# A spectral filter and two MLPs on one core: the first batch's loads and stores reordered, its filter loads cut to the rows in use

## Chip, cores, metric

The kernel runs on one core of a Trainium2 chip. The metric is the device time of one execution in microseconds. The two kernels are measured on the same chip; the median of three runs of the kernel before is 1429.06 us (1428.6 to 1431.17).

## What is computed

```python
# x: (4, 3136, 256) f32; filt: (1569, 256) complex
y = irfft(rfft(x, axis=1) * filt, n=3136, axis=1)        # filter over the sequence
u = y + real(fft(fft(y, axis=1), axis=2))                # 2-D transform mixed in
u = u + relu(norm(u) @ w1a) @ w2a                        # MLP 1: 256 -> 1024 -> 256
out = u + relu(norm(u) * g @ w1b) @ w2b                  # MLP 2: 256 -> 1024 -> 256
```

`norm` subtracts the mean of a token's 256 features and divides by their standard deviation. All of it is float32.

## The kernel before

The sequence transform of length 3136 = 64 x 49 is done in two stages that meet in device memory. The first stage (`over_p`, a generator that yields after each step) multiplies x by a 128x128 constant in 13 steps: load x (L254), one product on TensorE (L302), copy out of PSUM on ScalarE (L332, into `gst`), store to the scratch tensor `g` in device memory (L333). The second stage (`over_q`) runs over 17 groups of frequencies. In its tick t it loads a piece of `g` (L265, tile `gr`), multiplies it by the second constant (L302, and from t = 2 on by a rotated copy, L408), multiplies by the filter on VectorE (L416, L418 or L420), adds on GpSimd (L422, writes `y`), takes differences (L458, writes `z`), and two ticks later does the inverse product (L302 with `y`) and the transposes (L439); ScalarE copies the results out (L444 or L446 into `vst`, L450) and stores `vst` (L373) to a second scratch tensor `v`. ScalarE also multiplies one half of each filter tile by a sign (L368). After the last tick `v` is loaded back (L495) and 25 units of 512 tokens (`prep_ticks`, `ln_ticks`, `w1_step` L682, `w2_step` L705) follow. Batches 1 to 3 go through both stages in the gaps of the units of the batch before, so only batch 0's transform, the subject of the change, stands by itself at the start.

The filter of batch 0 comes in 17 loads (`load_f`, tile `fc`), 16 of 512 KB and one of 256 KB; each fills 128 partitions, of which 0 to 48 and 64 to 112 hold values and the other 30 zeros. The first three go to pool `fp`, the next two to pool `up` (which holds x before), the last 12 to the memory of the weights `w2a`, `w1b` and `w2b`, which are written only later. A filter is loaded four ticks before its use, a piece of `g` three before.

The weights come as 64-bit words and are made into two float32r halves by `conv_ticks` in chunks of 512 columns: a load (L636, tile `ww`), three masks and two combining steps on VectorE (L665 to L667, L651, L653), three copies on ScalarE (L658, L659, L219) and two steps on GpSimd (L655, L220). One "a" step of the schedule moves the first three chunks of `w1a` on by one of these stations.

The order is written out by hand: every engine runs its instructions in the order in which the program issues them. `DURING` says after which half tick of `over_q(0)` which other steps are issued: `a` as above, `k` a load of constants (L730), `c` the other weight chunks, `s` the split of constants, `x` the loads of batch 1's x, `f` a step of batch 1's first stage. `P0` does the same during `over_p(0)`.

Loads are issued by SyncE (SP) in that order; `vst` is stored by ScalarE. A DMA raises one of eight semaphores, which are given out in turn, in program order, over both issuing engines. Before an engine issues a DMA it waits until the last one on the same semaphore has landed, so at most eight are under way, and an engine whose next DMA has to wait issues nothing behind it.

Of the kernel before, what the change touches and what calls it, by code (L numbers as in the profile page):

```python
# [9 lines left out]
F32 = mybir.dt.float32  # L10
F32R = mybir.dt.float32r
I32 = mybir.dt.int32
ACTF = mybir.ActivationFunctionType
# [4 lines left out]
B, S, D, H = 4, 3136, 256, 1024  # L18
# [109 lines left out]
NA, LAG = 3, 3  # L128
N1 = 8
AHEAD, XW = 4, 7  # L130
WHEN = (-1, -1, 0, 1, 3, 3, 4, 5)
DURING = {0: 'aa', 2: 'a', 6: 'a', 14: 'k', 16: 'a', 30: 'cs', 33: 'x', 35: 'ff', 36: 'sf', 37: 'cc', 39: 'f', 40: 'f'}
P0 = {9: 'a'}
AFTER = "ppcfspfcppfpfppfpppc"
CONV = (0, 1, 3, 6, 9, 11, 12, 14, 15, 17, 19, 20, 21, 22, 23, 24, 25, 26, 27, 28)
P1 = (2, 3, 4, 5, 7, 8, 9, 10, 10)
# [11 lines left out]
def spectral_mlp_kernel(ctx: ExitStack, tc, x, ff, cst, w1a, w2a, gln, w1b, w2b, out):  # L148
    nc = tc.nc
# [107 lines left out]
    def pairs(t):  # L257
        return t.rearrange("(j p) d -> p j d", p=128)
# [3 lines left out]
    def load_g(b, c):  # L262
# [2 lines left out]
        nc.sync.dma_start(out=t[:98], in_=src)  # L265
        g_raw[b, c] = t[:98]

    def load_f(b, i, eng=nc.sync):
        k0, k1 = XCH[i]
        nk = k1 - k0  # L270
        if b == 0 and i > 2:
            if i < 5:
                t = up.tile([128, 4, D], F32, tag="u", name="fc").rearrange("p a d -> p (a d)")
            else:
                j = i - 5
                if j % 4 == 0:
                    f_tile[0] = wp.tile([128, 4096], F32, tag="w" + ("2a", "1b", "2b")[j // 4], name="fc")
                t = f_tile[0][:, j % 4 * 1024:j % 4 * 1024 + 1024]
            t = t.rearrange("p (a t d) -> p a t d", t=2, d=D)
            eng.dma_start(out=t[:, :nk], in_=ff[:, k0:k1])  # L280
            f_sb[b, i] = t[:, :, 0], t[:, :, 1]
        else:
            t = fp.tile([128, 2, 2, D], F32, tag="f", name="fc")
            eng.dma_start(out=t[:, :nk], in_=ff[:, k0:k1])
            f_sb[b, i] = t[:, :, 0], t[:, :, 1]
# [19 lines left out]
    def over_p(b):  # L305
# [7 lines left out]
        def exact(c):  # L313
            return b == 0 or b == 1 and c < N1
# [5 lines left out]
        def store():  # L320
            k, n, ps = done.pop()
            if b == 0 and k % 5 > 2:
                st = vrp.tile([128, 2, D], F32, tag="vr", name="gst")
            elif b == 1 and exact(k):
                if k % 2:
                    st = tp.tile([128, 2, D], F32, tag="t2", name="gst")
                else:
                    st = hp.tile([128, 512], F32R, tag="hl", name="gst").bitcast(F32)
                    st = st.rearrange("p (a d) -> p a d", d=D)
            else:  # L330
                st = stg.tile([128, 2, D], F32, tag="st", name="gst")
            nc.scalar.activation(out=st[:, :n], in_=ps[:, :n], func=ACTF.Copy)  # L332
            (nc.sync if exact(k) else nc.scalar).dma_start(out=pairs(g_dram[b][k * 256:k * 256 + n * 128]), in_=st[:, :n])  # L333

        for c in range(NC):
            if c + 3 < NC and (b, c + 3) not in x_raw:
# [386 lines left out]
    with tc.manual_schedule():  # L723
        def load_consts(c0, c1):
            if c0 % 512 == 0:
                i = c0 // 512
                t = hp.tile([128, 512], F32R, tag="h" + "hhl"[i], name="cr").bitcast(F32)
                cf[i] = t
            t = cf[c0 // 512][:, c0 % 512:c0 % 512 + c1 - c0]
            nc.sync.dma_start(out=t, in_=cst[:, c0:c1])  # L730
            return t
# [16 lines left out]
        def bufs_b(kind, i):  # L748
# [9 lines left out]
                return flat(yp.tile([128, 2, D], F32, tag="y", name="wm"))  # L758
            return flat(zp2.tile([128, 2, D], F32, tag="z", name="we"))

        load_consts(0, 128)
        p0 = over_p(0)
        for c in range(XW):
            load_x(0, c)
        cv = conv_ticks(["1a"], bufs_a, lambda i: -1 if i < 2 else 1, 0, NA)
        run(cv, 1)
        for c in range(XW, 13):
            load_x(0, c)
        run(p0, 1)
        load_consts(128, 512)  # L770
        nc.sync.dma_start(out=ctail, in_=cst[:, nw - 128:nw - 128 + ctail.shape[1]])
        nc.sync.dma_start(out=g_sb, in_=gln)
        ar = zp2.tile([128, 2, D], F32, tag="z", name="ar")[:, 0]
        nc.sync.dma_start(out=ar, in_=cst[:, NCONST - D - 128:NCONST - 128])
        turned[0] = xnp.tile([128, D], F32, tag="xn", name="f2s")[:, :128]
        nc.sync.dma_start(out=turned[0], in_=cst[:, NCONST - 128:])
        cs = consts()
        q0 = over_q(0)
        k = 0
        while run(p0, 1):  # L780
            k += 1
            for what in P0.get(k, ""):
                run(cv, 1)
        load_f(0, 0)
        load_consts(512, 1024)
        for what in DURING.get(0, ""):
            run(cv, 1)
        nc.scalar.activation(out=alt, in_=ar, func=ACTF.Copy)
        nc.scalar.activation(out=zmid, in_=ar, func=ACTF.Copy, scale=0.0)
        p1 = over_p(1)  # L790
        act = {
            "a": lambda: run(cv, 1),
# [8 lines left out]
        k = 0  # L801
        while run(q0, 1):
            k += 1
            for what in DURING.get(k, ""):
                act[what]()
        load_v(0)
        p = prep_ticks(0)
        for what in AFTER:
            act[what]()
# [2 lines left out]
        nc_ = sum(v.count("c") for v in (*DURING.values(), AFTER))  # L812
        assert nf >= 2 + N1
        assert sum(v.count("s") for v in (*DURING.values(), AFTER)) == 3
        assert sum(v.count("a") for v in DURING.values()) + sum(map(len, P0.values())) >= NA + LAG


        blocks = [(0, 0)]
# [156 lines left out]
```

## Time and profile before

| what | value |
|---|---|
| median of 3 runs | 1429.06 us |
| the profiled execution | 1427.74 us |
| its span (first to last instruction) | 1425.9 us |
| TensorE matmul busy | 1384.6 us, 97% of the span |
| VectorE, ScalarE, GpSimd busy | 885.6, 622.7, 408.3 us |
| data moved by DMA | 123.66 MB, mean 87 GB/s |

The prediction's sum is made in the profiled execution; its own time lies 1.84 us above its span and 1.32 us below the median. Busy times are averages over stages that have different limits: TensorE is idle for 41 us in all, and nearly all of that lies in the first tenth of the span, where the DMA engines are busy throughout.

### The profile page before, as it was taken

Reading aid. Unit: us, or ns where it says so; the run is one execution under the profiler, and the core shown is the slowest. Engines: PE = TensorE matmul, PEld = TensorE weight load, DVE = VectorE, ACT = ScalarE, POOL = GpSimd, SP = SyncE. Lnnn points to the kernel's source line nnn. Section 1 sums busy time; section 2 is a strip of 40 time slices with the busy share of each in tenths; the row PEclk is TensorE's granted clock in tenths of the full one; section 3 lists DMA queues with packets and bytes.
Section 4 is the critical chain, followed back from the end, with each engine's and each line's share of the span. In section 5 each row is a group of like instructions: output and inputs, shape, how many; then the busy total and the mean of one; then the engine's idle time right before and its main releaser. Section 6 shows DMA issues by size and latency. Waiting matters only on the chain.

```text
span 1425.9 us, 22918 instructions
## 1 busy us (share of the span) xinstructions
PE 1384.6 (97%) x8835; PEld 1221.6 (86%) x8835; DVE 885.6 (62%) x1814; ACT 622.7 (44%) x1350; POOL 408.3 (29%) x361
## 2 busy tenths in 40 slices
PE   4978999999999999999999999999999999999998
PEld 2437899888989999898999998898999999999998
DVE  2779977777554775767545666667555555555453
ACT  4755545645444544545344355445333233323222
POOL 1635534535231333434032244334100010100000
PEclk7988999999999999999999999999999999999999
DMA  9973332422233313312233233131000000000000
GB/s 325 316 272 108 102 99 83 141 78 85 77 115 124 97 49 114 109 48 68 68 103 118 77 90 114 42 114 62 19 30 30 31 1 31 30 15 16 30 15 23
DMA packets 65981, 123.66 MB, mean 87 GB/s; under 512 B 6096, under 2 KB 32848, under 8 KB 65872
## 3 DMA queue, kind: packets, MB, share of 16 engines
q1 hardware_dynamic: 49920, 99.00, 21.6%
q10 hardware_dynamic: 15952, 23.20, 5.0%
q8 instruction: 69, 1.13, 0.3%
q14 instruction: 40, 0.33, 0.1%
HBM read 83.12 MB, written 39.06 MB: 86 GB/s over the span
## 4 chain that ended last, share of the span: by engine, by line
PE 88%; DVE 5%; DMA 1%; issue 1%; ACT 0%; POOL 0%; ACTq 0%; POOLq 0%; DVEq 0%
PE ps L705 37%; PE ps L682 36%; PE ps L216 11%; PE ps L611 3%; DMA vd<-vst 1%; PE ps L439 1%; DVE we L651 1%; DVE wm L653 0%; DVE hl L688 0%; DVE wm L666 0%; DVE ww L667 0%; DVE xn L602 0%; PE ps L549 0%; POOL rs L598 0%; PE ps L302 0%
## 5 line engine op out<-in xcount | busy, mean ns | idle before, releaser
L687 ACT ACTIVATE hh<-ps 128x512 fp32r<-128x512 f32 (+1 forms) x400 | 235.4, 589 | 689.3 <-PE ps L682 666.9
L688 DVE SCALAR_TENSOR_TENSOR hl<-ps,hh 128x512 fp32r<-128x512 f32 (+1 forms) x400 | 271.7, 680 | 424.5 <-ACT hh L687 423.3
L682 PE MATMUL ps<-xth,w1a 128*128 128x512 f32 (+1 forms) x800 | 247.0, 391 | 0.0
L682 PE MATMUL ps<-xth,w1b 128*128 128x512 f32 (+1 forms) x800 | 243.7, 386 | 0.0
L705 PE MATMUL ps<-w2a,hh 128*128 128x256 f32 x1568 | 221.3, 283 | 2.0 <-ACT hh L687 2.0
L705 PE MATMUL ps<-w2b,hh 128*128 128x256 f32 x1568 | 218.3, 281 | 0.0
L705 PEld LDWEIGHTS ps<-w2b,hh 128*128 128x128 f32 x1568 | 206.2, 188 | 10.5
L705 PEld LDWEIGHTS ps<-w2a,hh 128*128 128x128 f32 x1568 | 205.3, 189 | 10.9 <-ACT hh L687 2.4
L598 POOL TENSOR_TENSOR rs<-rs,mhalf 128x4 f32<-128x4 f32 (+1 forms) x51 | 50.4, 988 | 413.8 <-DVE rs L597 405.6
L682 PE MATMUL ps<-xtl,w1a 128*128 128x512 f32 (+1 forms) x400 | 156.4, 391 | 0.0
L682 PE MATMUL ps<-xtl,w1b 128*128 128x512 f32 (+1 forms) x400 | 155.7, 389 | 0.0
L682 PEld LDWEIGHTS ps<-xth,w1a 128*128 128x128 f32 x800 | 136.8, 190 | 18.0 <-ACT xth L219 0.5
L682 PEld LDWEIGHTS ps<-xth,w1b 128*128 128x128 f32 x800 | 135.2, 188 | 16.5
L705 PE MATMUL ps<-w2a,hl 128*128 128x256 f32 x784 | 123.4, 279 | 3.8 <-DVE hl L688 3.8
L705 PE MATMUL ps<-w2b,hl 128*128 128x256 f32 x784 | 122.0, 277 | 0.1
L422 POOL TENSOR_TENSOR y<-y,t 128x512 f32<-128x512 f32 (+1 forms) x67 | 87.2, 1302 | 99.8 <-DVE t L420 85.7
L705 PEld LDWEIGHTS ps<-w2a,hl 128*128 128x128 f32 x784 | 104.9, 189 | 4.3 <-DVE hl L688 4.3
L705 PEld LDWEIGHTS ps<-w2b,hl 128*128 128x128 f32 x784 | 103.9, 188 | 0.3 <-DVE hl L688 0.3
L220 POOL TENSOR_TENSOR sl<-gr,sh 98x512 fp32r<-98x512 f32 x48 | 63.3, 1318 | 109.7 <-ACT sh L219 107.8
L220 POOL TENSOR_TENSOR sl<-y,sh 128x512 fp32r<-128x512 f32 (+1 forms) x51 | 67.2, 1317 | 79.9 <-issue 59.1
L682 PEld LDWEIGHTS ps<-xtl,w1a 128*128 128x128 f32 x400 | 75.8, 190 | 15.1
L682 PEld LDWEIGHTS ps<-xtl,w1b 128*128 128x128 f32 x400 | 75.3, 188 | 14.4
(115 smaller groups left out, 2040.6 us busy)
## 6 DMA issues: line engine op xcount, KB each, us to landing
fc<-in_ff SPq DMA_DIRECT2D x61, 512.0 KB
vd<-vst ACTq DMA_DIRECT2D x64, 200.0 KB
gr<-gd SPq DMA_DIRECT2D x64, 196.0 KB
xr<-in_x SPq DMA_DIRECT2D x48, 256.0 KB
vr<-vd SPq DMA_DIRECT2D x48, 256.0 KB
out<-u SPq DMA_DIRECT2D x24, 512.0 KB
gd<-gst ACTq DMA_DIRECT2D x28, 256.0 KB
gd<-gst SPq DMA_DIRECT2D x20, 256.0 KB
```

The source lines that it names most:

```text
L216: nc.tensor.matmul(out=o, lhsT=lhs[a], rhs=rhs[b], start=start and i == 0, stop=stop and i == 2)
L220: (lo_eng or nc.vector).tensor_tensor(out=lo, in0=src, in1=f32(hi), op=ALU.subtract)
L422: (nc.gpsimd if b or t < n - 1 else nc.vector).tensor_tensor(out=y[:, :nk], in0=y[:, :nk], in1=t2[:, :nk], op=ALU.add)
L439: nc.tensor.transpose(zp[:, a].rearrange("p t k -> p (t k)"), z[:, a], ident)
L598: nc.gpsimd.tensor_tensor(out=rs[:, tl], in0=rs[:, tl], in1=mhalf[:, tl], op=ALU.pow)
L611: nc.tensor.transpose(ps[:, t * 128:t * 128 + 128], xs[t][:, k * 128:k * 128 + 128], ident)
L651: nc.vector.scalar_tensor_tensor(out=p, in0=w[:, :, 1], scalar=-0x80000000, in1=p, op0=ALU.bitwise_and, op1=ALU.bitwise_or)
L682: nc.tensor.matmul(out=ps[:, :n], lhsT=w[:, a, k, m * 128:m * 128 + 128], rhs=xt[s][:, k, :n], start=i == 0, stop=i == 5)
L687: nc.scalar.activation(out=h[:, :n], in_=ps[:, :n], func=ACTF.Relu)
L688: nc.vector.scalar_tensor_tensor(out=l[:, :n], in0=ps[:, :n], scalar=0.0, in1=f32(h[:, :n]), op0=ALU.max, op1=ALU.subtract)
L705: nc.tensor.matmul(out=o[:, t % 2], lhsT=a[:, t * 128:t * 128 + 128], rhs=w[:, b, m], start=m == 0 and i == 0 and t % 2 == 0, stop=m == 7 ...
```

## The change

Five edits, all in batch 0's transform and its surroundings:

- All 13 loads of x are issued first; before, two loads of `w1a` (512 KB each) stood between the seventh and the eighth. The constants `ar` (128 KB) and `g_sb`, loaded before the stores of `g`, are now loaded during the second stage's fourth tick, and the two copies of `ar` (`alt`, `zmid`) stand after the second stage.
- The 13 stores of `g` of batch 0 are issued by ScalarE, right behind the copies that they store. Before, SP issued them behind all loads of x and of constants.
- Each filter load of batch 0 becomes three DMAs: rows 0 to 47, rows 64 to 111, and rows 48 and 112. The other rows are set to zero in the kernel, by GpSimd for the first five tiles and by VectorE once for the rest.
- The last 12 filters share one memory of four slots (that of `w2a`) and reuse them, where each had a place of its own.
- The conversion of the first three chunks of `w1a` begins in the second stage's first tick; before, it began ahead of the first stage's end. A load of chunk 2 that stood ahead of the loads of `g` now stands at the second stage's sixth tick.

```diff
--- before.py
+++ after.py
-DURING = {0: 'aa', 2: 'a', 6: 'a', 14: 'k', 16: 'a', 30: 'cs', ...}
-P0 = {9: 'a'}
+DURING = {3: 'a', 9: 'a', 12: 'a', 14: 'k', 15: 'a', 18: 'a', 22: 'a', 26: 'a', 29: 'cs', ...}
+    def rest(t, eng):
+        for r in (32, 96):
+            eng.memset(t[r:r + 32], 0.0)
+
+    def rows(t, src):
+        for r in (slice(0, 48), slice(64, 112), slice(48, 113, 64)):
+            nc.sync.dma_start(out=t[r], in_=src[r])
+
     def load_f(b, i, eng=nc.sync):
         k0, k1 = XCH[i]
         nk = k1 - k0
         if b == 0 and i > 2:
             if i < 5:
                 t = up.tile([128, 4, D], F32, tag="u", name="fc").rearrange("p a d -> p (a d)")
+                rest(t, nc.gpsimd)
             else:
-                j = i - 5
-                if j % 4 == 0:
-                    f_tile[0] = wp.tile([128, 4096], F32, tag="w" + ("2a", "1b", "2b")[j // 4], name="fc")
-                t = f_tile[0][:, j % 4 * 1024:j % 4 * 1024 + 1024]
+                j = (i - 5) % 4
+                t = f_tile[0][:, j * 1024:j * 1024 + 1024]
             t = t.rearrange("p (a t d) -> p a t d", t=2, d=D)
-            eng.dma_start(out=t[:, :nk], in_=ff[:, k0:k1])
+            rows(t[:, :nk], ff[:, k0:k1])
+            f_sb[b, i] = t[:, :, 0], t[:, :, 1]
+        elif b == 0:
+            t = fp.tile([128, 2, 2, D], F32, tag="f", name="fc")
+            rest(t.rearrange("p a t d -> p (a t d)"), nc.gpsimd)
+            rows(t[:, :nk], ff[:, k0:k1])
             f_sb[b, i] = t[:, :, 0], t[:, :, 1]
         else:
...
-            (nc.sync if exact(k) else nc.scalar).dma_start(out=pairs(g_dram[b][k * 256:k * 256 + n * 128]), in_=st[:, :n])
+            (nc.sync if b and exact(k) else nc.scalar).dma_start(out=pairs(g_dram[b][k * 256:k * 256 + n * 128]), in_=st[:, :n])
...
         load_consts(0, 128)
         p0 = over_p(0)
-        for c in range(XW):
+        for c in range(13):
             load_x(0, c)
-        cv = conv_ticks(["1a"], bufs_a, lambda i: -1 if i < 2 else 1, 0, NA)
-        run(cv, 1)
-        for c in range(XW, 13):
-            load_x(0, c)
+        f_tile[0] = wp.tile([128, 4096], F32, tag="w2a", name="fc")
+        rest(f_tile[0], nc.vector)
         run(p0, 1)
         load_consts(128, 512)
         nc.sync.dma_start(out=ctail, in_=cst[:, nw - 128:nw - 128 + ctail.shape[1]])
-        nc.sync.dma_start(out=g_sb, in_=gln)
-        ar = zp2.tile([128, 2, D], F32, tag="z", name="ar")[:, 0]
-        nc.sync.dma_start(out=ar, in_=cst[:, NCONST - D - 128:NCONST - 128])
         turned[0] = xnp.tile([128, D], F32, tag="xn", name="f2s")[:, :128]
         nc.sync.dma_start(out=turned[0], in_=cst[:, NCONST - 128:])
+        load_f(0, 0)
         cs = consts()
         q0 = over_q(0)
-        k = 0
-        while run(p0, 1):
-            k += 1
-            for what in P0.get(k, ""):
-                run(cv, 1)
-        load_f(0, 0)
+        run(p0)
+        run(q0, 1)
         load_consts(512, 1024)
-        for what in DURING.get(0, ""):
-            run(cv, 1)
-        nc.scalar.activation(out=alt, in_=ar, func=ACTF.Copy)
-        nc.scalar.activation(out=zmid, in_=ar, func=ACTF.Copy, scale=0.0)
+        cv = conv_ticks(["1a"], bufs_a, lambda i: -1 if i < 2 else 1, 0, NA)
...
         while run(q0, 1):
             k += 1
+            if k == 8:
+                ar = xnp.tile([128, D], F32, tag="xn", name="ar")
+                nc.sync.dma_start(out=ar, in_=cst[:, NCONST - D - 128:NCONST - 128])
+                nc.sync.dma_start(out=g_sb, in_=gln)
             for what in DURING.get(k, ""):
                 act[what]()
         load_v(0)
+        nc.scalar.activation(out=alt, in_=ar, func=ACTF.Copy)
+        nc.scalar.activation(out=zmid, in_=ar, func=ACTF.Copy, scale=0.0)
         p = prep_ticks(0)
```

How this moves instructions, at three places. First SP, behind the last store of batch 0's `g`, before (`gd` is `g` in device memory, `gr` a piece of it, `fc` a filter, `cr` a constant, `ww` a chunk of weight words):

```order
L284 DMA fc_233<-in_ff 128x1024
L730 DMA cr_235<-in_cst 128x512
L636 DMA ww_237<-in_w1a 128x1024
L265 DMA gr_260<-gd_155 98x512
L265 DMA gr_262<-gd_155 98x512
L265 DMA gr_264<-gd_155 98x512
L284 DMA fc_266<-in_ff 128x512
L284 DMA fc_268<-in_ff 128x1024
L280 DMA fc_270<-in_ff 128x1024
L280 DMA fc_292<-in_ff 128x1024
L265 DMA gr_308<-gd_155 98x512
```

and now, behind the first three loads of `g`, which follow the first filter directly (the stores are on ScalarE):

```order
L274 DMA fc_238<-in_ff 48x512 x2
L274 DMA fc_238<-in_ff 2x512
L274 DMA fc_244<-in_ff 48x1024 x2
L274 DMA fc_244<-in_ff 2x1024
L274 DMA fc_250<-in_ff 48x1024 x2
L274 DMA fc_250<-in_ff 2x1024
L742 DMA cr_256<-in_cst 128x512
L274 DMA fc_270<-in_ff 48x1024 x2
L274 DMA fc_270<-in_ff 2x1024
L648 DMA ww_276<-in_w1a 128x1024
L648 DMA ww_278<-in_w1a 128x1024
L264 DMA gr_294<-gd_154 98x512
```

The loads of `g` no longer stand behind a constant and a chunk of weights; the fifth filter (`fc_270`) and two chunks of `w1a` now stand ahead of the fourth load of `g` (`gr_294`).

Second GpSimd at the same place, before (`w1a` and `we` belong to the weights, `y` to the second stage's first ticks):

```order
L655 TENSOR_TENSOR we_201<-we_201,we_200 128x512
L220 TENSOR_TENSOR w1a_274<-we_201,w1a_274 128x512
L655 TENSOR_TENSOR we_242<-we_242,we_241 128x512
L422 TENSOR_TENSOR y_285<-y_285,t2_286 128x512
L422 TENSOR_TENSOR y_296<-y_296,t2_297 128x256
L220 TENSOR_TENSOR w1a_274<-we_242,w1a_274 128x512
L655 TENSOR_TENSOR we_252<-we_252,we_251 128x512
L422 TENSOR_TENSOR y_321<-y_321,t2_322 128x512
```

and now:

```order
L201 MEMSET mhalf_122 128x4
L270 MEMSET fc_159 32x1024 x2
L270 MEMSET fc_238 32x1024 x2
L270 MEMSET fc_244 32x1024 x2
L270 MEMSET fc_250 32x1024 x2
L434 ISA
L434 TENSOR_TENSOR y_263<-y_263,t2_264 128x512
L270 MEMSET fc_270 32x1024 x2
L434 TENSOR_TENSOR y_282<-y_282,t2_283 128x256
```

The zero rows of the fifth filter (`fc_270`) are set behind the addition of tick 0, and the DMAs of that filter wait for them.

Third SP in ticks 3 to 5 of the second stage, with the semaphores that each DMA waits for (DMAHW are those of earlier DMAs), before:

```order
L265 DMA gr_366<-gd_155 98x512 [waits DMAHW0_49,PE_49]
L280 DMA fc_310<-in_ff 128x1024 [waits DMAHW2_49]
L265 DMA gr_393<-gd_155 98x512 [waits DMAHW3_49,PE_49]
L280 DMA fc_310<-in_ff 128x1024 [waits DMAHW4_49]
L265 DMA gr_420<-gd_155 98x512 [waits DMAHW6_49,PE_49]
L280 DMA fc_422<-in_ff 128x1024 [waits DMAHW7_49]
L730 DMA cr_424<-in_cst 128x512 [waits DMAHW1_49]
```

and now:

```order
L264 DMA gr_353<-gd_154 98x512 [waits DMAHW7_49,PE_49]
L274 DMA fc_151<-in_ff 48x1024 [waits DMAHW0_49]
L274 DMA fc_151<-in_ff 48x1024 [waits DMAHW2_49]
L274 DMA fc_151<-in_ff 2x1024 [waits DMAHW3_49]
L264 DMA gr_387<-gd_154 98x512 [waits DMAHW4_49,PE_49]
L274 DMA fc_151<-in_ff 48x1024 [waits DMAHW5_49]
L274 DMA fc_151<-in_ff 48x1024 [waits DMAHW6_49]
L274 DMA fc_151<-in_ff 2x1024 [waits DMAHW0_49]
L648 DMA ww_409<-in_w1a 128x1024 [waits DMAHW1_49]
L264 DMA gr_425<-gd_154 98x512 [waits DMAHW2_49,PE_49]
```

The third part of the filter in the fourth row (DMAHW3) and the third chunk of `w1a` (`ww_409`, DMAHW1) wait for semaphores last held by ScalarE's stores of `vst` in ticks 4 and 5. Five DMAs a tick share the eight semaphores where there were three.

## Rows read from the trace of the kernel before

**Rows 1.** Busy time by stretch: stages of batch 0, then the rest.

```profile
core 0: us, PE busy (x) PEld busy (x) DVE busy (x) ACT busy (x) POOL busy (x), PEclk, DMA share, GB/s
2.00:26.20 24.20, 13.83 (x26) 5.90 (x26) 3.51 (x8) 10.24 (x20) 1.27 (x1) 0.87 1.02 343
26.20:31.90 5.70, 0.01 (x1) 0.04 (x1) 0.99 (x3) 1.75 (x4) 1.27 (x1) 0.50 1.01 321
31.90:42.50 10.60, 9.44 (x24) 5.17 (x24) 9.90 (x16) 5.24 (x15) 6.29 (x6) 0.75 1.02 331
42.50:78.70 36.20, 36.20 (x104) 16.23 (x104) 25.11 (x42) 26.79 (x79) 20.83 (x15) 1.00 0.97 327
78.70:105.90 27.20, 17.29 (x58) 9.40 (x56) 21.21 (x45) 14.67 (x34) 9.49 (x9) 0.87 0.75 259
160.00:1420.00 1260.00, 1256.91 (x8337) 1140.43 (x8336) 772.97 (x1619) 531.28 (x1138) 340.68 (x302) 1.00 0.21 67
```

**Rows 2.** Timeline of TensorE: start, duration, what [idle before <- who ended it].

```profile
4.14 13.83 PE L302 MATMUL ps<-xr,cr 128*128 128x512 f32 x26 [4.14 <-DMA xr<-in_x]
31.89 4.61 PE L302 MATMUL ps<-gr,cr 98*128 98x256 f32 x8 [13.92 <-DMA gr<-gd]
...
42.36 0.30 PE L439 MATMUL ps<-ctail,z 128*128 128x128 f32 x1 [1.05 <-DVE z L458]
42.50 1.02 PE L302 MATMUL ps<-gr,cr 98*128 98x512 f32 x2
...
45.30 1.02 PE L302 MATMUL ps<-gr,cr 98*128 98x512 f32 x2
...
84.38 0.44 PE L439 MATMUL ps<-ctail,z 128*128 128x128 f32 x2 [2.55 <-ACT z L462]
```

**Rows 3.** Timeline of SP's DMA issues.

```profile
1.18 3.27 SPq L254 DMA_DIRECT2D xr<-in_x  x7
...
14.75 8.89 SPq L333 DMA_DIRECT2D gd<-gst  x13
23.69 0.67 SPq L284 DMA_DIRECT2D fc<-in_ff  x1
...
26.19 1.53 SPq L265 DMA_DIRECT2D gr<-gd  x3
```

**Rows 4.** DMA issues in 0 to 30 us, with the size of each.

```profile
xr<-in_x SPq DMA_DIRECT2D x12, 256.0 KB
gd<-gst SPq DMA_DIRECT2D x12, 256.0 KB
...
ww<-in_w1a SPq DMA_DIRECT2D x3, 512.0 KB
```

**Rows 5.** GpSimd: timeline row; two groups with duration ns min/median/max.

```profile
36.15 2.06 POOL L422 TENSOR_TENSOR y<-y,t 128x512 f32<-128x512 f32 x2 [1.39 <-DVE t L420]
```

```profile
L533 POOL CAST zmid<-zsh x2: 386/386/387, 88.3 to 112.7; 1x256 fp32r<-1x256 f32 x2
L202 POOL MEMSET mhalf<- x1: 101/101/101, 0.7 to 0.7; 128x4 f32 x1
```

**Rows 6.** Busy time by stretch around TensorE's idle time at the second stage's end.

```profile
84.00:86.00 2.00, 1.62 (x4) 0.81 (x5) 0.23 (x1) 1.52 (x6) 0.00 (x0) 0.75 0.59 218
86.00:88.00 2.00, 2.00 (x4) 0.95 (x3) 0.78 (x3) 1.95 (x6) 0.00 (x0) 0.50 0.74 216
```

**Rows 7.** Chain of waits: start, duration, what; two stores of `vst`.

```profile
68.54 7.16 DMA vd<-vst
...
75.77 6.32 DMA vd<-vst
```

**Rows 8.** ScalarE: timeline of the copies of `ar`; the stores' issue group.

```profile
24.87 0.40 ACT L788 ACTIVATE alt<-ar 128x256 fp32r<-128x256 f32 x1
25.17 0.40 ACT L789 ACTIVATE zmid<-ar 128x256 fp32r<-128x256 f32 x1
```

```profile
L333 ACTq DMA_DIRECT2D gd<-gst x31: 344/366/404, 128.5 to 776.2; - x31
```

More of the change, by code (lines that the diff above doesn't have):

```diff
@@ L131 @@
 WHEN = (-1, -1, 0, 1, 3, 3, 4, 5)
-DURING = {0: 'aa', 2: 'a', 6: 'a', 14: 'k', 16: 'a', 30: 'cs', 33: 'x', 35: 'ff', 36: 'sf', 37: 'cc', 39: 'f', 40: 'f'}
-P0 = {9: 'a'}
+DURING = {3: 'a', 9: 'a', 12: 'a', 14: 'k', 15: 'a', 18: 'a', 22: 'a', 26: 'a', 29: 'cs', 32: 'x', 34: 'ff', 35: 'sf', 36: 'cc', 38: 'f', 39: 'f'}
 AFTER = "ppcfspfcppfpfppfpppc"
@@ L814, in spectral_mlp_kernel @@
         assert sum(v.count("s") for v in (*DURING.values(), AFTER)) == 3
-        assert sum(v.count("a") for v in DURING.values()) + sum(map(len, P0.values())) >= NA + LAG
+        assert sum(v.count("a") for v in DURING.values()) >= NA + LAG
         blocks = [(0, 0)]
```

## The prediction

> **What bounds the kernel now.** I read the busy time by stretch first. From 160 us to 1420 us TensorE is busy for 1256.91 of 1260 us, with the clock at its upper level [rows 1]. What is gained or lost before passes through to the end one to one, and no edit touches anything behind it. All that counts is how early batch 0's transform is through.
>
> Its second stage has two parts. From 42.5 to 78.7 us TensorE is busy for 36.20 of 36.20 us; a tick takes 2.80 us (42.50 to 45.30 [rows 2]). There the DMA share of 0.97 [rows 1] costs nothing: TensorE sets the pace. Ahead of it TensorE does nothing for 13.92 us, until the first load of `g` lands [rows 2]. In that time the DMA engines are full: from 2 to 26.2 us they move 343 GB/s at a share of 1.02 [rows 1]. So the start of the second stage is bound by bytes, and by what stands in the queue ahead of the loads of `g`: SP issues them at 26.19 us [rows 3], TensorE starts at 31.89 us.
>
> **The change part by part.** The sum is made in the profiled execution (1427.74 us); the median of the runs is 1.32 us higher.
>
> *The earlier start.* Between 2 and 26.2 us 24.2 x 343 GB/s = 8.30 MB move. Now 12 x 262 KB + 131 KB = 3.28 MB of x and as much of `g` must move before `g` may be read [rows 4], 0.41 MB of constants and, in the same queues, the first filter of 0.40 MB: 7.37 MB. Two chunks of `w1a` (1.05 MB [rows 4]) and `ar` (0.13 MB) are gone. 7.37 MB at 343 GB/s take 21.5 us, so the bytes are through at 23.5 us, and with 0.5 us for the last store to land SP can issue the loads of `g` at 24.0 us. Bounds: 22.8 us if the filter is still waiting then (0.40 MB less), 26.2 us if ScalarE, which now copies (0.6 us) and issues (0.37 us [rows 8]) in turn and waits for a free semaphore, brings the stores out no sooner. The load itself meets an empty queue. The first load of x was issued at 1.18 us [rows 3] and used at 4.14 us [rows 2]: 2.96 us, of which 0.33 MB at 343 GB/s are 0.95 us and 2.0 us are fixed. A load of 0.20 MB takes 2.6 us, so TensorE starts at 26.6 us, **5.3 us earlier**. The 5.70 us that the load took before contain a filter, a constant and a chunk of weights, which SP issued from 23.69 us on [rows 3].
>
> *The new wait in tick 4.* The fourth load of `g` (`gr_294`) now stands on SP behind the fifth filter (`fc_270`) and two chunks of `w1a`. That filter waits for its zero rows, and GpSimd sets these behind the addition of tick 0. The addition began 36.15 - 31.89 = 4.3 us after TensorE's first product [rows 2, 5] and takes some 1.4 of the pair's 2.06 us [rows 5]: it ends at 26.6 + 5.6 = 32.2 us. The trace has no MEMSET of 32x1024. The shortest, of 4 elements, took 0.10 us; at the additions' pace (2.06 us for 512 and 256 elements) 1024 would take 2.75 us; a cast of 256 elements took 0.386 us [rows 5], which scales to 0.10 + 4 x 0.286 = 1.24 us. I take this one, since it too has one input at most. Two of them: the filter's second part is issued at 34.7 us. Behind it come 0.20 MB of filter, 1.05 MB of `w1a` and 0.20 MB of `g`: 4.4 us at 331 GB/s, with the fixed 2.0 us 41.1 us. Before, tick 4 began at 42.50 us, 10.6 us after the first product, 1.05 us of it idle [rows 2]. So of 5.3 us only 1.4 are left: the wait costs **3.9 us** (1.6 with MEMSETs of 0.10 us, 6.9 with 2.75 us).
>
> *The clock.* TensorE would be idle for some 5 us there. [...] I take **2.0 us**.
>
> *Shorter run-ahead.* A tick had three DMAs and has five, while eight may be under way. In ticks 4 and 5 SP now waits for the stores of `vst` to land before it issues a part of a filter or a chunk of `w1a`, and the next load of `g` stands behind it. That load is needed three ticks, 8.4 us, after the store. A store takes 3 us (2.0 fixed, 0.6 for 0.20 MB, and some queue) to 7.16 us [rows 7]. With 3 us, a chunk of 0.52 MB (1.6 us), 0.8 us of issues and 2.6 us for the load: 8.0 us, which just fits; with 4.4 us, as I take it in a busy queue, 1.0 us is missing. A constant behind the store of tick 6 adds another wait, and ticks 7 to 9 lose **2.0 us** (0 to 6). Later ticks have no chunk between: 4.4 + 1.2 + 2.6 = 8.2 of 8.4 us.
>
> *The rest.* The filters are 30 of 128 rows smaller, 2.03 MB or 6.2 us of DMA time at 327 GB/s; it lies under TensorE's 36.20 us and is counted at nothing. If TensorE's pace were gone as cover it would be a gain. Converting `w1a` now lies wholly in the second stage, where VectorE is free for 11, ScalarE for 9 and GpSimd for 15 of 36.2 us [rows 1]: nothing, at most 1.5 us where a step stands ahead of a product's reader. VectorE and GpSimd have no other work before the first product when they set the other zero rows: nothing. [...] The two copies of `ar` move to ScalarE's path between the second stage and the first unit; they start 0.30 us apart and take 0.40 us each [rows 8]: **0.6 us** (0 to 0.8). The next loads of `w1a`, `w2a` and x come later on SP too; in 78.7 to 105.9 us TensorE is idle for 9.9 us anyway [rows 1], and I put **0.3 us** (a gain of 1.5 to a loss of 2).
>
> Sum: 5.3 - 3.9 - 2.0 - 2.0 - 0.6 - 0.3 = -3.5. The profiled execution would take 1431.2 us, the runs **1432.6 us**.
>
> The third part of each filter is 8 KB; I price it at one issue on SP, 0.4 us, inside the 0.8 and 1.2 us above. [...] No row here has a load of two rows.
>
> **The rivals.** *Faster: tick 4 does not wait.* If `gr_294` lands within 9.4 us of the first product, where TensorE came free (at 41.31 us, ahead of its idle 1.05 us [rows 2]), the clock stays up and the later waits find slack. That needs 4.9 of the 14.5 us between first product and landing to go, by a quicker start of the queue behind GpSimd and quick MEMSETs. Then 5.3 + 1.0 - 0.9 = 5.4 us are won: 1423.7 us. For it speaks that DMA has less to do; against it the order of GpSimd and SP, which is fixed. 0.17. *Same:* the loads of `g` start at 22.8 us and the MEMSETs take 0.10 us, or ticks 7 to 9 lose nothing: 1.2 + 2.3 = 3.5 us or 2.0 us better, 1429 to 1430.6 us. 0.17. *Slower still: the stores pace the stage.* With 7.16 us per store [rows 7] three ticks take 7.16 + 1.2 + 2.6 = 11.0 instead of 8.4 us, 0.87 us a tick, over 12 ticks 10 us: 1443 us. It decides from 4.6 us per store on. Against it: those 7.16 us were measured with 512 KB filters in the queue at a share of 0.97. 0.06. The change may also not start the stage earlier (26.2 us): 1434.8 us, within my case.
>
> **How the numbers follow.** My case (new waits eat the earlier start) has 0.60, with a range of its own from 1428.5 to 1437 us; some 0.43 of it lies above 1431.9 us. A measurement of this kernel can tell about 0.2%, 2.86 us, from no change. Faster: the first rival with a small part of the second, 0.18. Slower: 0.43 and 0.06, 0.49. Same: 0.33. The range reaches from the fast rival, 1423 us, to 1437 us, and leaves out the slow rival.
>
> **What would show it.** Right: first product of `gr` near 26.6 us; TensorE idle for 4 to 6 us before tick 4, ended by a load of `g`, and the clock at half behind it; SP waiting for GpSimd's MEMSET and for `vd`; ticks of 2.80 us from tick 10 on. Wrong: tick 4 directly behind tick 3, ticks longer than 2.80 us throughout, or MEMSETs that end long before tick 0.

## The result, and the profile after

| | before | after |
|---|---|---|
| median | 1430.12 us (1428.60 to 1431.44, 4 runs) | **1445.31 us** (1441.46 to 1445.82, 4 runs) |
| profiled execution, its span | 1427.74, 1425.9 us | 1445.82, 1443.9 us |
| first product with `g` | 31.89 us | 26.59 us |
| first product of unit 0 (`w1_step`) | 105.85 us | 124.97 us |

The ratio is 1.011 (95% interval 1.0094 to 1.0127): slower by some 15 us, where 1432.6 us was forecast, 3.5 us over the median of before at that time, with 1437 us as the upper end. The direction was right, the size far off. The profiled execution of the changed kernel is the slowest of its four, 18.1 us over the profiled one before; what is read from it below explains these 18.1 us, 2.9 more than the medians differ by.

The stage starts 5.3 us earlier, and batch 1's first product, which follows its last `g`, comes 20 us later (98.94 against 78.87 us). TensorE's timeline of the changed kernel (start, duration, what, [idle before <- who ended it]), against [rows 2]:

```profile
26.59 4.61 PE L314 MATMUL ps<-gr,cr 98*128 98x256 f32 x8 [9.70 <-DMA gr<-gd]
...
44.48 2.05 PE L314 MATMUL ps<-gr,cr 98*128 98x512 f32 x2 [7.31 <-DMA gr<-gd]
...
57.20 1.10 PE L314 MATMUL ps<-gr,cr 98*128 98x512 f32 x2 [2.23 <-DMA gr<-gd]
...
68.49 1.93 PE L314 MATMUL ps<-gr,cr 98*128 98x512 f32 x2 [2.59 <-DMA gr<-gd]
...
90.80 1.10 PE L314 MATMUL ps<-gr,cr 98*128 98x512 f32 x2 [2.15 <-DMA gr<-gd]
```

All of these waits are ended by a load of `g`; they go on to the last ticks, and the six ticks from 68.49 to 90.80 us take 3.72 us on average instead of 2.80. The same stretches as in [rows 1]:

```profile
31.90:42.50 10.60, 3.72 (x14) 1.99 (x13) 6.06 (x11) 4.83 (x16) 5.61 (x6) 0.94 0.73 202
42.50:78.70 36.20, 28.36 (x62) 11.54 (x62) 23.23 (x33) 18.23 (x51) 15.93 (x11) 0.83 0.72 198
180.00:1440.00 1260.00, 1256.99 (x8338) 1140.36 (x8336) 771.57 (x1616) 530.41 (x1136) 339.70 (x301) 1.00 0.21 67
```

From 42.5 to 78.7 us TensorE is busy for 28.36 instead of 36.20 us, at a granted clock of 0.83, while DMA is less busy (0.72 instead of 0.97) and moves 198 instead of 327 GB/s. Fewer bytes do not explain that: the loads of `g` that TensorE waits for come late although the DMA engines have time. Behind 180 us nothing has changed. The twelve ticks from tick 4 to tick 16, first before, then now:

```profile
42.50:76.07 33.57, 33.57 (x97) 15.14 (x97) 22.98 (x39) 24.77 (x73) 18.92 (x14) 1.00 0.97 325
44.48:94.79 50.31, 41.34 (x96) 17.32 (x97) 33.14 (x49) 27.57 (x77) 25.89 (x18) 0.87 0.76 212
```

They take 16.7 us longer: 9.0 us in which TensorE is idle (7.9 of them ended by a load of `g`) and 7.8 us because as many products run at a lower clock. What SP waited for from 20 to 95 us (total, times, longest):

```profile
SPq L274 <- DMA vd<-vst: 11.9, 5, 3.7
SPq L264 <- DMA gd<-gst: 6.4, 4, 4.1
SPq L274 <- DMA ww<-in_w1a: 4.8, 2, 4.3
SPq L274 <- DMA fc<-in_ff: 4.0, 4, 2.1
SPq L274 <- POOL fc L270: 3.8, 2, 3.2
SPq L742 <- DMA vd<-vst: 2.9, 1, 2.9
SPq L648 <- DMA vd<-vst: 1.8, 1, 1.8
```

L274 is a part of a filter, L742 a constant, L648 a chunk of weights. They wait for stores of `vst` to land, 16.6 us in these rows; behind them stand the next loads of `g`. Before, SP waited for such stores too,

```profile
SPq L280 <- DMA vd<-vst: 5.6, 3, 2.8
SPq L265 <- DMA vd<-vst: 3.2, 2, 1.9
```

and TensorE waited for none of the loads of `g` behind them: they had time. The chain of waits of the changed kernel has these stores in it, as [rows 7] had (issue to landing):

```profile
37.52 9.92 DMA vd<-vst
...
55.71 6.47 DMA vd<-vst
...
62.65 5.71 DMA gr<-gd
...
86.30 4.65 DMA vd<-vst
```

### The profile page after: what moved, and what is told of

Read it like the earlier page. It is cut to its first block, busy times and chain, and to the rows that moved or that the text cites. A ratio compares the mean times of both kernels' runs of the same rounds, so it can differ in the third digit from the quotient of the medians.

```text
span 1443.9 us, 23008 instructions
## 1 busy us (share of the span) xinstructions
PE 1390.1 (96%) x8835; PEld 1221.7 (85%) x8835; DVE 896.3 (62%) x1816; ACT 622.7 (43%) x1350; POOL 418.9 (29%) x371
## 4 chain that ended last, share of the span: by engine, by line
PE 87%; DVE 5%; DMA 3%; issue 1%; ACT 1%; POOL 0%; SPq 0%; ACTq 0%; DVEq 0%; POOLq 0%
PE ps L717 36%; PE ps L694 36%; PE ps L215 10%; PE ps L623 3%; DMA vd<-vst 1%; PE ps L451 1%; DVE we L663 1%; PE ps L314 1%; DMA gr<-gd 1%; DVE ww L679 1%; DVE wm L665 0%; DVE hl L700 0%; DMA xr<-in_x 0%; DVE xn L614 0%; DVE wm L678 0%
```

## The experiments

Seventeen kernels were run, the kernel before beside each group (its medians 1427.6 to 1429.0 us, 1430.1 us beside the change). Since these medians differ, kernels of different groups are compared by what each lies above the kernel before beside it: 15.2 us for the change. Two theories were there at first: A, that three loads a filter use up the eight semaphores, so that SP waits for stores of `vst`; C, that the stalls come from what now stands ahead of the loads of `g`. B (slow 8 KB parts) and D (four filter places) were its rivals.

### Undoing parts of the change

**Whole filters**, one load each (and no MEMSET):

```diff
-        for r in (slice(0, 48), slice(64, 112), slice(48, 113, 64)):
-            nc.sync.dma_start(out=t[r], in_=src[r])
+        nc.sync.dma_start(out=t, in_=src)
```

> The changed kernel, but each filter of batch 0 is one load of 128 rows again and nothing is set to zero. The early x, the stores by ScalarE, the late weights and the four filter places stay. Theory A (the loads in three parts use up the eight semaphores: five DMAs a tick, SP waits for stores of vst, TensorE for g): back to 1422 to 1428 us, the second stage of batch 0 at 2.80 us a tick, no idle time over 1 us ended by a load of g behind tick 5. Theory B (the 8 KB parts are slow transfers): the same here. Theory C (two chunks of w1a ahead of the fourth load of g, and later ones among the filters): tick 4 still waits and so do ticks 7 and 9, 1438 us or more. Theory D (four filter places instead of twelve): SP waits for products to free a place, ticks over 2.80 us behind tick 9, 1435 us or more.

Measured: 1431.91 us (1430.22 to 1436.33), ratio 1.0021 (1.0009 to 1.0033). Some 12 of the 15.2 us are the split's. But what is left of the change, which by the prediction's sum should gain, costs 3 us, and theory A's 1422 to 1428 us are missed too: TensorE still waits for `g` at four ticks behind tick 5, 1.47 us at the longest.

**Three parts that hold all rows**: `slice(0, 48), slice(48, 96), slice(96, 128)`, no MEMSET.

> The changed kernel with each filter loaded in three parts of 48, 48 and 32 rows, so all 128 rows come from memory, nothing is set to zero, and no part is under 131 KB. Five DMAs a tick as in the changed kernel, a third more bytes of filters. Theory A (number of DMAs): as slow as the changed kernel, 1440 to 1450 us, with TensorE waiting for loads of g by 2 us and more at several ticks. Theory B (8 KB parts): 1424 to 1430 us. Theory C (weights in the queue): 1438 to 1446 us with the waits at the same ticks 4, 7 and 9.

Measured: 1447.94 us, ratio 1.0126 (1.0109 to 1.0144). The 8 KB parts and the zero rows are not needed for the loss; as its only cause, B falls.

**Two parts**: `slice(0, 48), slice(64, 112)`.

> The changed kernel without the third part of each filter load: rows 48 and 112 of batch 0's filters are left out (they stay zero), so one frequency of 49 is not filtered. Four DMAs a tick, none under 190 KB, two MEMSETs per place as before. Theory A (number of DMAs): about half way back, 1430 to 1438 us, with eight DMAs now two ticks of work. Theory B (8 KB parts): 1424 to 1430 us. Theory C (weights in the queue): 1438 to 1446 us.

Measured: 1439.04 us, ratio 1.0069 (1.0044 to 1.0094): four DMAs a tick, some third of the way back (10.1 us are left of 15.2). That is 1 us above theory A's range and inside C's; and since the 8 KB part is gone together with a DMA, the run does not tell the two apart.

**The order mended**: `DURING = {5: 'a', ...}` instead of `{3: 'a', ...}`, and the fifth filter's MEMSETs issued with the fourth's.

> The changed kernel with the first two chunks of w1a behind the fourth load of g instead of ahead of it, and the fifth filter's zero rows set together with the others, ahead of tick 0's addition on GpSimd. Theory C (what stands ahead of the fourth load of g starts the stalls): tick 4 no longer waits over 2 us, the clock stays up, 1430 to 1436 us. Theory A: tick 4 gains its 4 to 7 us, the later ticks still wait for g as SP waits for stores, so 1437 to 1443 us.

Measured: 1442.20 us, ratio 1.0087 (1.007 to 1.0103). Tick 4 began without a wait at 41.02 us instead of 44.48, yet only 2 us come back (13.2 are left of 15.2): TensorE then waited for loads of `g` at ticks 5, 6 and 9, for 0.80, 2.64 and 3.25 us. C explains the first stall, not the loss.

### The split by itself, and two versions meant to be better

**The kernel before with three parts** (only that):

```diff
-            eng.dma_start(out=t[:, :nk], in_=ff[:, k0:k1])
+            for r in (slice(0, 48), slice(48, 96), slice(96, 128)):
+                eng.dma_start(out=t[r, :nk], in_=ff[r, k0:k1])
```

> The kernel before with one edit: each filter of batch 0 in three loads of 48, 48 and 32 rows instead of one of 128. Same bytes, same places, same order, nothing set to zero. Theory A (the number of DMAs a tick sets how far SP runs ahead): slower by 10 to 20 us, 1439 to 1450 us, SP waiting for stores of vst and TensorE for loads of g as in the changed kernel. If the early start, the late weights or the four places are needed for the loss: 1428 to 1433 us.

Measured: 1442.94 us, ratio 1.0094 (1.0077 to 1.0111). This one edit costs as much as the whole change. Some 2 us of it lie ahead of the stage: the first product with `g` comes at 33.94 instead of 31.89 us.

**Whole filters in twelve places** instead of four:

> The changed kernel with whole filters (one load each) and twelve places again instead of four. Against it stands the run with whole filters in four places, 1431.91 us, where SP waited 10.0 us in all for VectorE to free a place. Theory D (places): these waits go and the early start of 4.4 us comes through, 1424 to 1428 us. Theory E (bytes: the stage starts earlier, but w1a, ar and the filters must come through it at a DMA share of 0.84 to 0.99): the loads of g are as late as with four places, 1430 to 1434 us.

Measured: 1431.99 us, ratio 1.0028 (1.0016 to 1.004). The waits for a free place are gone, the time is the same; D falls.

**Pairs**: the twelve later filters two at a time, in fewer and larger parts.

```diff
+            r = slice(0, 48) if i % 2 else slice(64, 112)
+            nc.sync.dma_start(out=t[r], in_=ff[r, k0:k0 + 4])
```

> The changed kernel with the zero rows still left out, but in fewer DMAs: filters 5 to 16 are loaded two at a time (rows 0 to 47 of a pair in one tick, rows 64 to 111 in the next, 0.39 MB each), rows 48 and 112 of four filters in one load ahead of the stage, twelve places, the first five filters whole, and the chunks of w1a behind the fourth load of g. Some 3 DMAs a tick as in the kernel before, a quarter less bytes for twelve filters. Theories A and E both: the ticks run at 2.80 us, no wait for g over 1 us behind tick 5, and the early start comes through, 1421 to 1427 us. Theory B (thin loads are slow wherever they stand) or a bound that neither names: 1430 us or more.

Measured: 1444.06 us, ratio 1.011 (1.0095 to 1.0125). A clear miss: three DMAs a tick and fewer bytes, and no better than the change. Its row of the busy time by stretch (columns as in [rows 1]):

```profile
42.00:82.00 40.00, 28.54 (x65) 11.66 (x62) 26.84 (x39) 20.23 (x57) 18.22 (x13) 0.87 0.90 204
```

DMA is busy at a share of 0.90 and moves 204 GB/s. Before, 0.97 stood beside 327 GB/s [rows 1]. So besides the number of DMAs there is a second effect: the same share of DMA time moves less. This is theory F below. The first effect is not gone, though: SP waits for stores of `vst` for 29 us here, more than in any other run, so this run does not part the two.

### What kind of part

**Parts of spread rows**: `slice(0, 128, 2), slice(1, 128, 4), slice(3, 128, 4)` in the kernel before.

> The kernel before with each filter in three loads again, but of every second row (64 rows) and of every fourth row (32 and 32), so that each load reaches over all 128 partitions. Number of DMAs, bytes and row size (4 KB) are those of the run in which rows 0 to 47, 48 to 95 and 96 to 127 were loaded apart (1442.94 us against 1427.56). Theory A (number of DMAs a tick against eight semaphores): slow all the same, 1439 to 1448 us. Theory F (loads that fill only a third of the partitions move slower, about 200 GB/s where whole ones move 330): 1427 to 1432 us, rows of 4 KB back at some 170 to 210 ns each.

Measured: 1443.78 us, ratio 1.0095 (1.0071 to 1.012).

**Parts by columns**, each of all 128 rows:

```diff
+        for c in (slice(0, nk * 256), slice(nk * 256, nk * 384), slice(nk * 384, nk * 512)):
+            eng.dma_start(out=dst[:, c], in_=src[:, c])
```

> The kernel before with each filter in three loads of all 128 rows, split along the row: 2 KB, 1 KB and 1 KB of each row's 4 KB. Five DMAs a tick and the same bytes, in smaller rows. Theory A (number of DMAs): 1439 to 1448 us. Theory F (partitions reached): 1427 to 1433 us. If only the rows' size counts (1 and 2 KB packets), this one is slower than the one with every second row.

Measured: 1433.28 us, ratio 1.0027 (1.0014 to 1.004). The two contradict both theories taken alone: spread rows are slow though they reach all partitions, columns nearly as fast as whole loads though there are as many DMAs. What SP waited for, first with spread rows, then with columns:

```profile
SPq L281 <- DMA vd<-vst: 13.7, 5, 4.6
SPq L640 <- DMA vd<-vst: 4.2, 1, 4.2
SPq L265 <- DMA vd<-vst: 2.6, 2, 2.1
```

```profile
SPq L265 <- DMA vd<-vst: 4.0, 2, 3.7
SPq L272 <- DMA vd<-vst: 2.4, 6, 0.5
SPq L645 <- DMA vd<-vst: 2.3, 1, 2.3
```

In these rows it waits 20.5 against 8.7 us for such stores. The difference is which load comes next on the semaphore of a store. Followed through the instructions (a load belongs to tick t if it stands behind the load of `g` issued in tick t), the load that waits for the store of tick t belongs to

| kernel | tick of the waiting load | median |
|---|---|---|
| before | t + 2 to t + 3 | 1429 us |
| three parts by columns | t + 1 | 1433 us |
| three parts by rows, contiguous or spread | t | 1443 us, 1444 us |
| the change | t - 1 up to tick 6, then t | 1445 us |
| pairs | t in ticks 3 and 4, then t + 1 to t + 2 | 1444 us |

Rows and columns have as many DMAs; what differs is where the stores stand among them. The first store is DMA number 57 with rows and 60 with columns, and a semaphore comes round again after eight DMAs. So the load of `g` issued in tick 6, for one, waits for the store of tick 6 with rows and for that of tick 5 with columns. Where the waiting load belongs to tick t or earlier, SP can run no further ahead than to the store of the tick that TensorE is in. Pairs do not fit: as slow, with a lag of one tick and more; there the slow movement comes on top. Whether the number of DMAs acts through this lag alone is the question of the next group.

**Spreading the conversion** (whole filters, twelve places; `DURING = {5: 'a', 10: 'a', 16: 'a', 20: 'a', 24: 'a', 28: 'a', 31: 'a', ...}`):

> Whole filters, twelve places, the early start, and the conversion of w1a moved: its first two chunks behind the fourth load of g, its seven steps spread to every fourth half tick, up to tick 15, instead of crowded between ticks 4 and 13. Theory G (what eats the early start of the whole-filter runs is VectorE: with the conversion beside it, z took 1.50 us instead of 0.47 us, and TensorE waited for it): 1424 to 1428 us. Theory E (bytes): 1430 to 1434 us as with the crowded conversion, 1431.99 us.

Measured: 1432.51 us, ratio 1.0025 (1.0012 to 1.0038): no gain.

### The stores of `vst` taken off the shared semaphores

GpSimd's DMAs have semaphores of their own (DMASW0 to 7 in the instructions, not DMAHW0 to 7). One edit,

```diff
-            nc.scalar.dma_start(out=dst, in_=vst[0][:NV])
+            (nc.scalar if b else nc.gpsimd).dma_start(out=dst, in_=vst[0][:NV])
```

in the changed kernel:

> The changed kernel with batch 0's stores of vst issued by GpSimd instead of ScalarE, so that they have semaphores of their own and no load on SP waits for one of them. Nothing else changes: three parts, 8 KB parts, order, places. Theory A' (SP's loads wait for stores of vst whose semaphore they reuse, and the loads of g stand behind them): SP's 18 us of waits for vd go, 1430 to 1436 us. Theory F (the parts themselves move slowly): 1442 us or more, TensorE still waits for g by 2 us at several ticks. Half and half would be 1437 to 1440 us.

Measured: 1437.43 us (1436.56 to 1440.26), ratio 1.006 (1.0037 to 1.0084): 9.0 us over the kernel before instead of 15.2, so some 6 us come back, the case that was called half and half. But for the one that reads `v` back (0.3 us), no load on SP waits for `vd` any more (it waits 10.9 us for VectorE to free a filter's place instead), and TensorE's timeline has no wait of over 1 us for `g` behind tick 4:

```profile
45.31 2.05 PE L314 MATMUL ps<-gr,cr 98*128 98x512 f32 x2 [7.35 <-DMA gr<-gd]
63.37 0.41 PE L451 MATMUL ps<-ctail,z 128*128 128x128 f32 x2 [1.81 <-DVE z L470]
68.29 0.41 PE L451 MATMUL ps<-ctail,z 128*128 128x128 f32 x2 [1.93 <-DVE z L470]
```

In the kernel before with three contiguous parts:

> The kernel before with three loads of 48, 48 and 32 rows a filter (1442.94 us) and the stores of vst issued by GpSimd. Theory A': 1429 to 1434 us. Theory F: 1440 us or more, since rows of 4 KB still take some 250 ns and DMA moves 240 GB/s.

Measured: 1435.47 us, ratio 1.0048 (1.0034 to 1.0062), between the two forecasts: 7.0 us over the kernel before instead of 15.4. And in the kernel before alone:

> Control: the kernel before with the stores of vst issued by GpSimd and nothing else. Both theories: 1427 to 1433 us; what it lies above the kernel before is the price of issuing on GpSimd, whose additions stand behind the issues.

Measured: 1427.31 us, ratio 0.9993 (0.9982 to 1.0004): the move itself, which also puts the stores into another queue, costs nothing.

For the half that stays, the other two kinds of parts with the same edit:

> The kernel before, each filter in three loads of all 128 rows (2, 1 and 1 KB of each row), the stores of vst issued by GpSimd. If the half that is left is slow movement into part of the partitions: 1426 to 1430 us, DMA over 300 GB/s in the second stage. If it is the number of DMAs: 1434 to 1437 us as with three parts by rows, 1435.47 us.

Measured: 1428.97 us, ratio 1.0012 (1.0000 to 1.0024).

> The kernel before, each filter in three loads of every second and every fourth row, the stores of vst issued by GpSimd. If slow movement comes from contiguous rows 0 to 47, 48 to 95 and 96 to 127 falling on the same paths: 1426 to 1431 us, rows of 4 KB at some 160 to 200 ns. If any load of fewer than 128 rows is slow: 1434 us or more.

Measured: 1429.13 us, ratio 1.0010 (1.0000 to 1.0019). All eight kernels with only the filters' loads and the stores' engine changed:

| each filter of batch 0 | stores by ScalarE | stores by GpSimd |
|---|---|---|
| one load | 1.0000 | 0.9993 |
| three, by columns | 1.0027 | 1.0012 |
| three, spread rows | 1.0095 | 1.0010 |
| three, contiguous rows | 1.0094 | 1.0048 |

In the right column the number of DMAs costs some 0.1%, at the edge of what these runs can tell; only contiguous parts cost more. The busy time from 42 to 82 us, first with contiguous parts and stores by GpSimd:

```profile
42.00:82.00 40.00, 33.79 (x91) 14.46 (x90) 22.35 (x37) 23.62 (x72) 26.06 (x26) 1.00 1.00 258
```

and with spread rows and stores by GpSimd:

```profile
42.00:82.00 40.00, 38.95 (x113) 17.50 (x112) 28.80 (x47) 29.27 (x88) 30.03 (x30) 1.00 1.00 333
```

Both have the DMA engines full, at as many DMAs of the same rows of 4 KB; what differs is which rows go together (and so the sizes of the parts: 48, 48, 32 rows against 64, 32, 32), and 258 stand against 333 GB/s. The same rows are read together from device memory; no run parts the reading side from the writing side. With the stores by ScalarE the two kinds were equally slow; there the DMA engines were not full from 42 to 82 us (shares of 0.86 and 0.78), so that the waits for stores set the pace.

### The early start

> Candidate: the early start, whole filters in twelve places, the conversion of w1a spread out, and the stores of vst issued by GpSimd. If the early start was lost to SP's waits for stores: 1422 to 1426 us, faster than both kernels. If it is lost to VectorE (the conversion beside the stage) or to bytes: 1428 to 1433 us.

Measured: 1434.40 us, ratio 1.0053 (1.0038 to 1.0068). Its first product with `g` comes at 28.17 us, but VectorE is full in places (third busy time in each row):

```profile
66.00:74.00 8.00, 7.24 (x21) 2.88 (x20) 7.62 (x11) 5.98 (x16) 7.98 (x8) 1.00 1.00 278
82.00:90.00 8.00, 5.55 (x16) 1.81 (x14) 7.96 (x10) 5.77 (x16) 6.20 (x8) 1.00 0.84 327
```

From 42 to 82 us as a whole it is busy for 33.93 of 40 us, and TensorE waits longer for loads of `g` there (4.2 us) than for `z` (1.2 us). It is no faster than with the stores by ScalarE, 1432.51 us: SP's waits for stores were not what ate the early start. The conversion was then moved behind tick 14 (`DURING = {24: 'a', 30: 'a', 31: 'a', 33: 'a', ...}`):

> The early start, whole filters in twelve places, the stores of vst issued by GpSimd, and the conversion of the first three chunks of w1a moved behind tick 14, so that none of it stands in the ticks before. Against it stands the same kernel with the conversion spread over ticks 4 to 15, 1434.4 us. Theory G (VectorE, slowed beside GpSimd, holds TensorE in the stage): no wait of TensorE for z between 45 and 80 us, ticks of 2.80 us, 1424 to 1431 us, what is won in the stage being partly paid behind it. Theory E (bytes, DMA share 1.0): waits for loads of g take the place, 1431 us or more.

Measured: 1442.59 us, ratio 1.0092 (1.0069 to 1.0115), a miss for the theory that VectorE is the only thing in the way. TensorE's longest waits:

```profile
74.05 2.05 PE L314 MATMUL ps<-gr,cr 98*128 98x512 f32 x2 [4.13 <-DMA gr<-gd]
91.69 0.66 PE L451 MATMUL ps<-ctail,z 128*128 128x128 f32 x2 [4.36 <-DVE z L470]
100.96 0.66 PE L451 MATMUL ps<-ctail,z 128*128 128x128 f32 x2 [6.90 <-DVE z L470]
```

Up to 74 us no wait for `z` is left, but loads of `g` are still late, by 4.13 us behind the first two chunks of `w1a`, and `z` is held up for 11.3 us behind that, while VectorE converts. Work and bytes that were done ahead of the stage have to go somewhere in it or behind it; no place that was tried is free.

## Why the prediction was wrong, step by step

- **What bounds the kernel; nothing changes behind 160 us.** Right: 1256.99 of 1260 us behind 180 us. Between the stage and there a part is taken back: the changed kernel is 20.1 us late at batch 1's first product, 19.1 at unit 0's, 18.1 at the end.
- **The earlier start, 5.3 us.** Right to the tenth: 26.59 us against 26.6. That it counts in full was wrong. With whole filters, where nothing else of the split is left, the stage starts 4.4 us earlier (27.45 us) and the kernel is 2.9 us slower. Of the 4.4 us only 1.4 are left at tick 4 (41.14 against 42.50 us): TensorE waits 1.07 us for a constant and its granted clock stays lower for longer (0.50 from 27.40 to 34.80 us, 0.74 from there to 46.00 us, against 0.75 from 31.90 to 42.50 us before [rows 1]). The ticks from 4 to 16 then take 39.7 instead of 33.6 us, with 3.5 us of waits for `g` and 1.3 us for `z`. The sum priced the conversion of `w1a` beside the stage at nothing; VectorE, free for 11 of 36 us by [rows 1], is then busy for 34.57 of 40 us (42 to 82 us). With twelve places one `z` took 1.50 instead of 0.47 us while a step of GpSimd ran (last section), but one took 1.52 us before the change too.
- **The new wait in tick 4, 3.9 us.** The mechanism was right, the size was not: tick 4 began at 44.48 instead of 41.1 us, after 7.31 us of idle time. The MEMSETs were faster than taken (1.94 us for two, 0.97 each, against 1.24). What was off is the rate: 1.45 MB were to move at 331 GB/s; DMA moved 239 GB/s from 34.8 to 46 us. 1.45 MB take 6.1 us at that rate, with the fixed 2.0 us 8.1, so that the load would land at 42.8 us: that is half of what was missing. The load itself was issued at 36.14 us and landed 8.3 us later; what held it for the rest is not shown. Mending the order gave back 2 us, no more, since later waits took its place.
- **The clock, 2.0 us.** Too small, since the stalls did not end at tick 4: the granted clock was 0.83 on average from 42.5 to 78.7 us, where it had been 1.00, and from tick 4 to tick 16 the products were busy for 41.34 instead of 33.57 us, 7.8 us. No run shows the 2.0 us as such; tick 4 of the changed kernel, behind its wait, took 4.68 us (44.48 to 49.16 us) instead of 2.80, at a granted clock of 0.50 up to 46.50 us and 0.59 from there to 48.50 us, 1.9 us more for this one wait.
- **Shorter run-ahead, 2.0 us. This is the step that failed.** The mechanism is the one named, SP waiting for stores of `vst`, but it was priced at ticks 7 to 9 alone, with the words that later ticks need 8.2 of 8.4 us. Measured, the store takes 4.65, 6.47 or 9.92 us to land and not 4.4, and the load of `g` behind it 5.71 us and not 2.6. 6.47 + 1.2 + 5.71 = 13.4 us do not fit into 8.4. Instead of 2.0 us at ticks 7 to 9, TensorE waited 7.9 us for loads of `g` from tick 7 to tick 15, and the clock's 7.8 us go with these waits. Taking the stores off the semaphores gave back some 6 us of the median; the slow parts (next point) share in the rest.
- **The filters' fewer bytes, counted at nothing.** They cost time, as far as the kernel before shows it: the parts move slowly. In the kernel before, contiguous parts cost 0.48% (7.0 us) with the stores' waits out of the way, spread ones 0.10%; the changed kernel's own parts were not run in another shape. From 42 to 82 us, with the stores by GpSimd, contiguous parts moved 258 GB/s and as many spread ones 333 GB/s, both at a DMA share of 1.00. Whether that lies in the rows that are filled, in the rows of device memory that are read together or in the sizes of the parts, no run shows. A part of 8 KB is not needed for the loss: three parts without one cost as much (1447.94 against 1445.31 us), at a third more bytes. What the thin part costs by itself stays open: without it, and so with one DMA less a tick, 5 us came back.
- **The copies of `ar` and the later loads, 0.9 us.** Nothing can be seen of them: from batch 1's first product to unit 0 it took 27.0 us before and takes 26.0 us now (98.94 to 124.97 us). VectorE's two MEMSETs, counted at nothing, took 3.47 us each and were over at 9.49 us, 17.1 us ahead of the first product with `g`.
- **The rivals.** "Slower still: the stores pace the stage", 1443 us, came nearest to the measured 1445.31 us and had a chance of 0.06. Against it stood that the 7.16 us of a store [rows 7] were measured with large filters in the queue. The stores of the changed kernel took 4.65 to 9.92 us with small ones. That its number comes so near is partly luck: it puts 10 us on the stores alone, which gave back some 6. And it was named as the only way to lose over 7 us; that contiguous parts can move less than spread ones (258 against 333 GB/s) was no case at all. The fast rival's 4.9 us to be saved are 5.1 by its own numbers (14.5 less 9.4); nothing hangs on it.

Put together, each against the kernel before beside it: the change is 15.2 us slower, 9.0 with the stores taken off the semaphores, 2.9 with whole filters. So whole filters give back some 12 us, about half of which are the stores' semaphores and the other half the rest of the split (slow parts, the wait for zero rows); the 2.9 us that remain are the early start with its work moved into the stage. The lines between these are not sharp, since one wait hides another, and what of the 2.9 us is VectorE, what DMA and what the clock stays open. No kernel that was run is measurably faster than the one before; 1427.31 us, stores by GpSimd, has an interval that includes no change.

## What to carry to other kernels

Where DMAs of two engines shared eight semaphores, splitting a load was paid here by the engine that waits for the other's DMAs: follow each semaphore to its next user and ask how long ago the DMA on it was issued; with a lag of one tick (columns) the kernel lost 4 us here that came back without the shared semaphores, with none (spread rows) 14 us; two to three ticks, as before, cost nothing. A load that leaves out unused rows saves bytes, but that need not be time: in contiguous parts it lost more than it saved here (15.2 us over the kernel before, 2.9 with whole filters), and a spread one that leaves out rows was not run. And an early start is worth what the next stage has free: price the work that is moved out of the way where it lands, on engines and DMA alike.

## What the runs showed of the hardware

That a full queue moves 258 GB/s with contiguous parts and 333 GB/s with spread ones, both at a share of 1.00, was not expected here. Nor was that one `z` of VectorE takes three times as long as another, in the kernel with whole filters in twelve places. Its VectorE, then its GpSimd:

```profile
64.14 0.47 DVE L470 SCALAR_TENSOR_TENSOR z<-y,ctail 128x254 f32<-128x254 f32 x1
...
66.61 1.76 DVE L665 SCALAR_TENSOR_TENSOR we<-ww,we 128x512 f32<-128x512 int32 x1
68.29 1.50 DVE L470 SCALAR_TENSOR_TENSOR z<-y,ctail 128x254 f32<-128x254 f32 x1
```

```profile
62.70 1.45 POOL L667 TENSOR_TENSOR we<-we 128x512 f32<-128x512 f32 x1
64.30 1.45 POOL L434 TENSOR_TENSOR y<-y,t 128x512 f32<-128x512 f32 x1
...
67.79 1.72 POOL L219 TENSOR_TENSOR w1a<-we,w1a 128x512 fp32r<-128x512 f32 x1
```

The `z` at 64.14 us takes 0.47 us; the step of GpSimd ahead of it ends at 64.15 us, and the next begins at 64.30 us, while it runs. The `z` at 68.29 us takes 1.50 us, with a step that began ahead of it and runs from 67.79 to 69.51 us; it ends 0.28 us behind that step. The kernel before has such a `z` too, 1.52 us from 53.56 us on, with a step of GpSimd from 53.52 to 54.80 us, 0.28 us ahead of its end. Why these take longer no run shows; none tried the step on another engine.
